# Splitting the last token products of a linear-attention block into a z part and a rest

## Chip, cores and metric

The kernel runs on one core of a Trainium2 chip. The metric is the device time of one launch in microseconds; the median over five runs of the kernel before the change is 197.4 us (196.29 to 198.48). A second number, the span, is the time between the first and the last instruction of one profiled execution; it is a little shorter than the time of the same run.

The engines are named as in the profile: PE is the matrix engine (PEld its weight loads), DVE the vector engine, ACT the scalar engine, POOL GpSimd, SP the engine whose queue issues the DMAs here.

## What is computed

A transformer layer on 2048 tokens of width 448: linear attention with 16 heads of 28, then a gated feed-forward part of width 1792. Both have a layernorm in front and a residual around them.

```python
qkv = (x_norm @ wqkv).reshape(B, S, 3, H, Dh)          # H = 16, Dh = 28
phi = lambda t: jnp.where(t > 0, t + 1, jnp.exp(t)) + 1e-6
pq, pk = phi(q), phi(k)
kv  = jnp.einsum("bhsd,bhse->bhde", pk, v)
z   = jnp.einsum("bhsd->bhd", pk)                      # sum of phi(K) over the tokens
num = jnp.einsum("bhqd,bhde->bhqe", pq, kv)
den = jnp.einsum("bhqd,bhd->bhq", pq, z)[..., None] + 1e-6
h   = x + (num / den) @ wo
h2  = h + (gelu(hn @ w_gate) * (hn @ w_up)) @ w_down   # hn = layernorm(h)
```

Softmax is absent, so all tokens share one 28x28 matrix per head (kv) and one vector z. Both are sums over all tokens: nothing of the attention's output can be formed before the last K tile has gone through phi.

## The kernel before

The 2048 tokens are 16 tiles of 128. Every tile passes through the same named steps; a number behind a name is its tile.

**First layernorm.** bnst1 and bnag1 (DVE) form mean and variance, ln1 and rstd1 (ACT) the reciprocal root, normD (DVE, tiles 0 to 3) or normP (POOL, the others) the normalised tile `xnn`, in a ring of six slots. Each slot is 512 wide: 448 columns of data and 64 columns that hold ones. Tiles 0 to 3 are transposed by PE (tr), the others by a DMA that SP issues (xT).

**Projections.** k and q are four matmuls of 448 columns each. ek, ck and pk (ACT, DVE, DVE) make phi(K), in a ring of four slots; eq and rq (ACT) are the exponential and the relu of Q, cq and aq (DVE) join them to phi(Q). K and Q share four PSUM banks in turn.

**Token products.** V is never formed. For every K tile, four matmuls accumulate xnn^T phi(K) into four banks (4 to 7), each with another 128 rows of xnn as weights (pt). The last of these, number 3, covers data columns 384 to 447 and the 64 columns of ones: its lower half is z, repeated over 64 partitions. For tiles 0 to 14 the four are one task (`pt4`), issued in the order 3, 0, 1, 2. For tile 15 there are two tasks: `pt1_15`, number 3 alone, and `pt3_15`, the other three.

**From the sums to gate/up.** z1 (ACT) and z0 (DVE) spread z over 128 partitions; evpA and evpD bring the four token products to SBUF; kv (PE, 16 matmuls) multiplies them by the V weights, kvm (DVE) masks the heads, w2 (PE, four) multiplies by wo, evwA and evwD evict. In parallel, per tile: t1 = phi(Q) * z (t1d on DVE for tile 0, t1p on POOL otherwise, two buffers), dr the sum over each head (DVE), deA the epsilon (ACT), rd the reciprocal (DVE), pn the scaled phi(Q) (DVE). Tiles 0 and 1 are then transposed on PE (tro, evicted by evo), the other pairs by a DMA (oT). out1 and out2 multiply by w2, hr (DVE) adds x. A second layernorm (bnst2, bnag2; ln2 and rstd2 on ACT for tiles 0 and 1, negm2, vpe2 and pow2 on POOL otherwise; nhD or nhP) and a transpose (trh for tiles 0 and 1, elsewhere wr64 or wrap on DVE and the DMA hT) give the input of the feed-forward part.

**Feed-forward.** gu2 and gu4 are groups of gate and up matmuls that fill one bank each; ge (ACT) is the gelu, hm (DVE) the product. down (14 matmuls of 448 columns) follows for each tile, fo (DVE) adds the residual and do (SP) writes out. The w_down load (`dwd`) is issued by SP among the transposes. The table of gelu is loaded on ACT (tbl2) after the last exponential of Q.

**Order.** The order of the tasks on each engine is not the order in which the program creates them. It is written out as five lists of task numbers (`ORDERS`, lines 15 to 51; PE, ACT, DVE, POOL, SP); `_Graph.place` (line 110) takes them and `_Graph.emit` (line 145) issues each engine's tasks in that order, with a semaphore wait for every dependence on another engine. An engine that waits holds up whatever stands behind in its list. Before the change, PE's list around the edit reads, by names: k_13 q_4 k_14 q_5 k_15 pt4_11 pt4_12 pt4_13 pt4_14 pt1_15 pt3_15 q_7 q_6 kv q_8 w2_1 w2_0 q_11 w2_3 q_9 w2_2 tro_0 q_10 tro_1 out1_0 out1_1 q_15 q_12 q_13 q_14 trh_0 trh_1 out2_2 gu2_0. DVE's after the last pk: aq_0 cq_4 aq_4 cq_5 aq_5 evpD_3 z0 t1d_0 evpD_2 dr_0 dr_1 rd_0 kvm dr_2 evwD_1 dr_3 rd_2 rd_1 pn_0 pn_1.

Lines of the code that appear in the profile: 407 the K and Q projections, 418 to 420 ek, ck, pk, 426 the token products, 434 and 435 eq and rq, 452 and 453 z1 and z0, 465 kv, 474 w2, 491 t1, 494 dr, 498 pn, 507 tro, 526 out, 532 hr, 553 trh, 563 wrap, 606 and 608 gate and up, 578 down, 626 ge, 628 hm.

Of the kernel before, what the change touches and what calls it, by code (L numbers as in the profile page):

```python
# [5 lines left out]
BF16 = mybir.dt.bfloat16  # L6
F32 = mybir.dt.float32
ALU = mybir.AluOpType
# [4 lines left out]


ORDERS = (
    "30 36 38 70 47 45 67 56 80 54 75 65 88 63 83 74 79 91 120 87 103 95 115 107 130 142 119 154 134 166 146 178"
    " 158 190 170 182 202 214 219 229 234 244 194 206 218 233 248 249 253 250 290 256 294 292 265 298 259 296 314"
    " 262 316 318 319 277 268 271 274 332 336 355 433 438 386 443 448 453 458 417 463 505 510 515 520 525 530 471"
    " 468 489 535 577 582 540 561 587 592 597 602 543 674 607 612 617 622 627 632 637 642 705 647 650 653 721 726"
    " 731 736 741 746 751 756 761 766 771 776 781 786 803 808 656 791 794 797 813 818 823 828 833 838 843 848 853"  # L20
    " 858 863 868 800 873 876 879 882 885",
    "4 29 33 34 37 42 43 51 52 71 46 69 60 61 55 76 68 98 64 90 99 84 125 89 110 126 111 81 92 82 137 138 149 104"
    " 150 161 162 116 185 173 121 131 174 122 143 186 197 224 155 225 198 167 209 239 210 179 240 191 203 215 230"
    " 221 245 235 220 236 284 287 288 254 255 252 307 251 258 311 346 293 266 297 350 315 257 267 317 264 260 261"
    " 278 326 327 263 328 329 378 382 272 279 333 270 273 275 276 269 338 413 436 434 409 439 441 446 444 449 451"
    " 454 456 461 459 464 466 508 506 511 481 513 516 485 518 523 521 526 528 533 553 531 557 536 538 670 666 580"
    " 578 585 583 590 588 593 595 697 600 605 598 603 701 608 610 613 615 620 618 625 623 630 628 633 635 640 638"
    " 645 643 722 724 727 729 732 734 737 739 742 744 747 749 752 754 757 759 762 764 767 769 772 774 777 779 782"
    " 784 787 789 804 806 809 811 816 814 821 819 824 826 829 831 834 836 839 841 846 844 849 851 854 856 861 859"
    " 869 871 864 866",  # L30
    "31 32 40 35 41 49 50 39 44 53 48 72 58 59 73 57 62 96 66 97 123 108 77 124 78 109 183 85 147 86 148 135 93 184"
    " 136 94 159 171 160 105 106 222 207 172 117 223 118 195 132 196 133 208 144 237 145 156 238 157 339 341 168 169"
    " 302 340 180 181 300 192 193 204 205 216 303 217 231 342 232 246 247 301 371 372 373 374 286 285 304 289 306"
    " 310 308 291 345 295 349 347 312 309 313 377 299 351 348 320 352 321 323 322 324 404 325 330 381 331 334 383"
    " 335 379 384 380 337 405 402 356 359 403 412 360 357 408 414 358 361 435 437 415 442 410 440 411 387 447 445"
    " 388 369 476 450 474 452 546 477 475 366 455 457 390 462 460 391 547 548 480 418 549 389 392 465 467 421 419"
    " 509 507 484 420 512 514 422 397 517 519 400 661 423 552 524 522 486 482 487 483 529 428 662 659 556 554 527"
    " 660 472 431 555 558 534 665 532 469 690 669 493 537 539 559 490 692 693 581 491 667 579 584 668 492 586 494"
    " 671 691 672 541 700 562 696 591 495 589 594 596 601 563 565 604 566 599 698 702 606 703 544 675 567 699 609"
    " 564 611 676 614 616 678 621 619 572 626 500 624 631 503 629 677 679 634 636 639 680 709 641 706 644 710 707"  # L40
    " 646 648 711 708 575 688 723 725 728 730 733 735 738 740 743 745 748 719 750 654 753 685 755 758 760 716 763"
    " 765 768 770 651 773 775 778 780 783 785 788 790 810 657 805 807 812 792 798 795 817 815 822 820 825 827 830"
    " 832 835 837 840 842 847 845 850 852 855 857 862 860 865 801 870 872 874 867 877 880 883 886",
    "17 24 0 18 1 23 27 19 2 25 21 22 100 101 112 127 113 128 139 140 151 152 163 187 164 175 176 28 226 199 188"
    " 211 200 212 227 241 26 242 20 305 343 344 375 376 407 406 362 363 364 365 368 478 479 393 394 395 399 550 396"
    " 425 426 424 427 551 430 663 664 695 694 497 498 496 499 502 569 570 568 571 574 682 681 683 687 712 713 714"
    " 718 684 715",
    "3 5 6 7 8 9 10 11 12 13 14 15 16 102 114 129 141 153 165 177 189 201 213 228 243 280 281 282 283 353 385 416"
    " 370 367 354 398 401 488 429 432 560 673 542 470 704 504 501 573 576 545 473 689 720 717 686 649 799 658 793"
    " 875 655 652 802 881 878 884 796 887",  # L50
)


# [117 lines left out]
def bass_sequential_preLN__linear_attn_block__glu_gated_geglu__prompt_kernel(  # L171
    nc, A_x, A_wqkv, A_wo, B_x, B_w_gate, B_w_up, B_w_down, out
):
    S, D, FF, H, DH = 2048, 448, 1792, 16, 28
    T, P = S // 128, S // 256
# [2 lines left out]
    FC = 768  # L178
    NJ = FF // 128
    EPS_LN, EPS = 1e-5, 1e-6  # L180
    XN_R, HN_R, HR = 6, 4, 8
    N_PE_TR = 4
    B1_CHUNKS = [2, 2, 4, 4, 4]
    WARM = 40
# [3 lines left out]
    G = _Graph()  # L188
    es = ExitStack()
    with es:  # L190
        block = es.enter_context(nc.Block())

        def sb(name, shape, dt):
            return es.enter_context(nc.sbuf_tensor(name, shape, dt))

        x_sb = sb("x_sb", [128, T, D], BF16)
        xnn = sb("xnn", [128, XN_R, 512], BF16)
# [23 lines left out]
        ln2 = sb("ln2", [128, T], F32)  # L221
        rs2 = sb("rs2", [128, T], F32)
        e1 = sb("e1", [128, 4, D], BF16)
        pk = sb("pk", [128, 4, D], BF16)
        eq = sb("eq", [128, T, D], BF16)
        pq = sb("pq", [128, T, D], BF16)
        pt_sb = sb("pt_sb", [128, 4, D], BF16)
# [14 lines left out]
        ps = es.enter_context(nc.psum_tensor("ps", [128, 8, 512], F32))  # L242
        psb = ps[:].bitcast(BF16)

        def bufs(name, n):
            return [_Buf("%s%d" % (name, i)) for i in range(n)]

        b_x = bufs("x", T)
        b_xn = bufs("xn", XN_R)
        b_xnT = [bufs("xnT%d_" % t, 2) for t in range(T)]  # L250
        b_ones2 = _Buf("ones2")
# [4 lines left out]
        b_epsd = _Buf("epsd")  # L256
        b_st1, b_mv1, b_nm1, b_ln1, b_rs1 = bufs("st1", T), bufs("mv1", T), bufs("nm1", T), bufs("ln1", T), bufs("rs1", T)
        b_st2, b_mv2, b_nm2, b_ln2, b_rs2 = bufs("st2", T), bufs("mv2", T), bufs("nm2", T), bufs("ln2", T), bufs("rs2", T)
        b_e1, b_pk = bufs("e1", 4), bufs("pk", 4)
        b_eq, b_pq = bufs("eq", T), bufs("pq", T)  # L260
        b_pt, b_z, b_kvm, b_w2 = bufs("pt", 4), bufs("z", 2), _Buf("kvm"), bufs("w2", NG)
        b_t1, b_den, b_rd = bufs("t1", 2), bufs("den", 4), bufs("rd", 4)
# [5 lines left out]
        b_ps = bufs("ps", 8)  # L268
# [3 lines left out]
        BK_PT = (4, 5, 6, 7)  # L272
# [15 lines left out]
        def op(eng, fn, r, w, name, after=()):  # L288
            return G.add(eng, fn, r=r, w=w, name=name, after=after)
# [47 lines left out]
        def act_exp(fn, r, w, name):  # L337
            t_ = G.add("act", fn, r=r, w=w, name=name, after=[tbl1])
            exps.append(t_)
            return t_  # L340
# [58 lines left out]
        def slot():  # L399
            slots[0] += 1  # L400
            return BK_S[slots[0] % 4]

        def proj(e, W, t, bk, w):
            ins = None
            for k in range(4):
                W(k)
                ins = e.matmul(ps[:, bk, 0:D], xnT[:, t, k, :], w[:, k, :], start=(k == 0), stop=(k == 3))  # L407
            return ins

        def proj_reads(t, b):  # L410
            return [(b_xnT[t][0], 0), (b_xnT[t][1], 2), (b[0], 0), (b[1], 3)]

        def k_tile(t):
            bk = slot()
            i = t % 4
            psK = ps[:, bk, 0:D]
            G.add("pe", lambda e, W: proj(e, W, t, bk, wk_sb), r=proj_reads(t, b_wk), w=[b_ps[bk]], name="k_%d" % t, mw=True)
            eks.append(act_exp(lambda e: e.activation(e1[:, i, :], psK, AF.Exp), [b_ps[bk]], [b_e1[i]], "ek_%d" % t))  # L418
            op("dve", lambda e: e.tensor_scalar(e1[:, i, :], e1[:, i, :], 1.0 + EPS, 0.0, ALU.min, ALU.max), [b_e1[i]], [b_e1[i]], "ck_%d" % t)
            op("dve", lambda e: e.scalar_tensor_tensor(pk[:, i, :], psK, EPS, e1[:, i, :], ALU.max, ALU.add), [b_ps[bk], b_e1[i]], [b_pk[i]], "pk_%d" % t)  # L420
            groups = ((3, 0, 1, 2),) if t < T - 1 else ((3,), (0, 1, 2))
            for cs in groups:
                def fpt(e, cs=cs):
                    ins = None
                    for c in cs:
                        ins = e.matmul(ps[:, BK_PT[c], 0:D], xnn[:, t % XN_R, c * 128:(c + 1) * 128], pk[:, i, :], start=(t == 0), stop=(t == T - 1))  # L426
                    return ins
                G.add("pe", fpt, r=[b_xn[t % XN_R], b_ones2, b_pk[i]], w=[b_ps[BK_PT[c]] for c in cs], name="pt%d_%d" % (len(cs), t))


        def q_tile(t):
# [6 lines left out]
        for what in SEQ.split():  # L438
            t = int(what[1:])
# [6 lines left out]
        for i in range(2):  # L446
            cs = slice(0, FC) if i == 0 else slice(FC, FF)
# [25 lines left out]
        for g in range(NG):  # L473
            G.add("pe", lambda e, g=g: e.matmul(ps[0:GW, BK_W2[g], 0:D], kvm[:, g, :], wo_sb[:, g, :], start=True, stop=True),
                  r=[b_kvm, b_wo], w=[b_ps[BK_W2[g]]], name="w2_%d" % g)
# [218 lines left out]
```

## Time and profile before

| what | us |
|---|---|
| median of five runs | 197.4 |
| time of the profiled execution | 197.96 |
| its span | 195.9 |
| PE busy in the span | 188.7 |
| DVE busy in the span | 132.7 |
| gate and up matmuls, line 606, busy (line 608 runs beside it) | 86.7 |
| down matmuls, line 578, busy | 43.4 |

Busy time by stretch of 5 us each:

| stretch, us | PE | DVE | ACT | POOL |
|---|---|---|---|---|
| 15 to 20 | 3.58 | 3.20 | 2.40 | 1.97 |
| 25 to 30 | 5.00 | 4.47 | 2.18 | 2.91 |
| 35 to 40 | 4.99 | 4.35 | 3.67 | 0.93 |
| 40 to 45 | 4.77 | 5.00 | 3.82 | 4.76 |
| 45 to 50 | 4.75 | 5.00 | 4.26 | 0.20 |
| 55 to 60 | 5.00 | 5.00 | 3.40 | 2.79 |
| 80 to 85 | 5.00 | 5.00 | 0.31 | 2.43 |
| 120 to 125 | 5.00 | 2.92 | 0.00 | 1.26 |

In a timeline each line gives the start, the duration, the engine, the source line, the operation, what it writes and reads, how many instructions are merged, and in brackets the idle time of the engine before it with what ended it. The ends of matmuls are modelled and overlap the next start, so a stop of PE is read from the distance between starts; the brackets show only part of it. The granted clock of PE is 1.00 in every stretch.

### The profile page before, as it was taken

The page shows a single profiled execution, that of the slowest core. Times are in us where ns is not written, and L with a number is a line of the kernel's source. Part 1 is how long each engine was busy: PE and PEld are TensorE (multiplying, and loading weights), DVE is VectorE, ACT ScalarE, POOL GpSimd, SP SyncE. Part 2 cuts the span into 40 slices and gives each one's busy share as a digit, 9 for nine tenths or more (in the row PEclk, how much of TensorE's full clock was granted, in tenths as well). Part 3 has the DMA queues.
Part 4 walks back from the last instruction along what each step waited for, and adds up shares of the span by engine and source line. Part 5 has one row for each costly group of instructions (what it writes and reads, how often), then busy time and mean ns, then how long its engine had stood idle before and what let it go on. Part 6 is the DMA issues. An engine that isn't in the chain of part 4 may idle for free.

```text
span 195.9 us, 4160 instructions
## 1 busy us (share of the span) xinstructions
PE 188.7 (96%) x1572; PEld 104.2 (53%) x1572; DVE 132.7 (68%) x355; ACT 77.4 (39%) x226; POOL 51.3 (26%) x93
## 2 busy tenths in 40 slices
PE   7897999999999999999999999999999999999995
PEld 7443455554468697554454635445343544555554
DVE  2896986899999999999777757045653405452422
ACT  3685754688992244222231440044444002443000
POOL 7043751092055475802430412510000000000000
DMA  5989254998222794922401176500350002000022
GB/s 156 290 270 93 60 107 98 231 215 172 54 57 56 119 308 94 95 56 54 100 3 30 25 70 76 132 12 0 62 106 0 0 0 74 0 0 3 0 95 94
DMA packets 35955, 16.97 MB, mean 87 GB/s; under 512 B 27744, under 2 KB 34656, under 8 KB 35936
## 3 DMA queue, kind: packets, MB, share of 16 engines
q1 hardware_dynamic: 35792, 16.60, 40.7%
q8 instruction: 12, 0.20, 0.4%
q10 hardware_dynamic: 144, 0.11, 0.2%
q14 instruction: 7, 0.06, 0.1%
HBM read 8.26 MB, written 1.84 MB: 52 GB/s over the span
## 4 chain that ended last, share of the span: by engine, by line
PE 82%; DVE 8%; DMA 5%; POOL 1%; ACT 1%; issue 1%; SPq 0%; DVEq 0%; POOLq 0%
PE ps L606 29%; PE ps L578 22%; PE ps L608 16%; PE ps L407 6%; PE ps L526 6%; PE ps L426 4%; DMA x_sb<-in_A_x_dram 3%; DMA xnT<-xnn 2%; DVE pqn L498 1%; DVE den L494 1%; DVE st L351 1%; DVE w L479 1%; DVE x_sb L532 1%; DVE pk L420 0%; PE ps L553 0%
## 5 line engine op out<-in xcount | busy, mean ns | idle before, releaser
L608 PE MATMUL ps<-hnT,wgu_sb 64*128 64x512 bf16 (+1 forms) x490 | 87.4, 334 | 0.0
L606 PE MATMUL ps<-hnT,wgu_sb 64*128 64x512 bf16 (+1 forms) x490 | 86.7, 334 | 0.2 <-issue 0.2
L626 ACT ACTIVATE gl<-ps 128x256 bf16<-128x256 f32 x112 | 37.0, 380 | 84.5 <-PE ps L608 81.0
L628 DVE TENSOR_TENSOR hh<-ps,gl 128x256 bf16<-128x256 f32 x112 | 43.4, 415 | 34.1 <-ACT gl L626 33.8
L606 PEld LDWEIGHTS ps<-hnT,wgu_sb 64*128 64x128 bf16 x490 | 44.1, 94 | 21.8 <-issue 2.7
L608 PEld LDWEIGHTS ps<-hnT,wgu_sb 64*128 64x128 bf16 x490 | 42.6, 94 | 15.0 <-DVE hh L628 5.0
L578 PE MATMUL ps<-wd_sb,hh 128*128 128x448 bf16 (+1 forms) x238 | 43.4, 342 | 0.0
L578 PEld LDWEIGHTS ps<-wd_sb,hh 128*128 128x128 bf16 x238 | 22.8, 98 | 20.4 <-issue 1.9
L491 POOL TENSOR_TENSOR t<-pq,zbc 128x448 f32<-128x448 bf16 x15 | 16.6, 1118 | 30.7 <-DVE pq L487 21.9
L351 DVE BATCH_NORM_STATS2 st<-x_sb 128x6 f32<-128x448 bf16 x32 | 19.2, 613 | 3.8 <-DMA x_sb<-in_A_x_dram 3.8
L582 DVE TENSOR_TENSOR x_sb<-ps,x_sb 128x448 bf16<-128x448 f32 (+1 forms) x17 | 10.0, 592 | 15.6 <-PE ps L578 15.6
L407 PE MATMUL ps<-wk_sb,xnT 128*128 128x448 bf16 x64 | 14.4, 353 | 1.9 <-DMA xnT<-xnn 1.4
L407 PE MATMUL ps<-wq_sb,xnT 128*128 128x448 bf16 x64 | 14.2, 353 | 0.3 <-ACT eq L434 0.3
L426 PE MATMUL ps<-pk,xnn 128*128 128x448 bf16 x64 | 13.9, 353 | 0.4 <-DVE pk L420 0.3
L526 PE MATMUL ps<-w,pqnT 112*128 112x448 bf16 x64 | 13.8, 353 | 0.1
L418 ACT ACTIVATE e<-ps 128x448 bf16<-128x448 f32 x16 | 8.7, 543 | 9.7 <-PE ps L407 9.7
L561 POOL TENSOR_SCALAR hn<-x_sb,nm,rs 128x448 bf16<-128x448 bf16 x14 | 11.5, 828 | 3.3 <-DMA hnT<-hn 2.7
L532 DVE TENSOR_TENSOR x_sb<-ps,x_sb 128x448 bf16<-128x448 f32 x16 | 9.7, 613 | 2.2 <-PE ps L526 2.2
L498 DVE TENSOR_TENSOR pqn<-pq,rd 128x448 bf16<-128x448 bf16 x16 | 11.1, 707 | 0.0
L391 POOL TENSOR_SCALAR xnn<-x_sb,nm,rs 128x448 bf16<-128x448 bf16 x12 | 8.6, 714 | 6.9 <-ACT rs L360 5.9
L420 DVE SCALAR_TENSOR_TENSOR pk<-ps,e 128x448 bf16<-128x448 f32 x16 | 9.9, 617 | 0.2
L407 PEld LDWEIGHTS ps<-wk_sb,xnT 128*128 128x128 bf16 x64 | 5.9, 97 | 7.7 <-issue 2.4
(68 smaller groups left out, 136.9 us busy)
## 6 DMA issues: line engine op xcount, KB each, us to landing
out_dram<-x_sb SPq DMA_DIRECT2D x15, 112.0 KB, 1.8
wd_sb<-in_B_w_down_dram SPq DMA_DIRECT2D x1, 1568.0 KB, 7.0
x_sb<-in_A_x_dram SPq DMA_DIRECT2D x3, 448.0 KB, 6.4
wgu_sb<-in_B_w_gate_dram SPq DMA_DIRECT2D x1, 896.0 KB, 11.9
wgu_sb<-in_B_w_up_dram SPq DMA_DIRECT2D x1, 896.0 KB, 15.8
wgu_sb<-in_B_w_gate_dram SPq DMA_DIRECT2D x1, 672.0 KB, 5.9
wgu_sb<-in_B_w_up_dram SPq DMA_DIRECT2D x1, 672.0 KB, 8.3
wo_sb<-in_A_wo_dram SPq DMA_DIRECT2D x1, 392.0 KB, 9.3
```

Of the source, the lines that this page charges most:

```text
L351: op("dve", lambda e: e.bn_stats(st[:, t, :], src_ap), [b_src], [b_st[t]], "bnst%s_%d" % (tag, t))
L407: ins = e.matmul(ps[:, bk, 0:D], xnT[:, t, k, :], w[:, k, :], start=(k == 0), stop=(k == 3))
L426: ins = e.matmul(ps[:, BK_PT[c], 0:D], xnn[:, t % XN_R, c * 128:(c + 1) * 128], pk[:, i, :], start=(t == 0), stop=(t == T - 1))
L491: op(eng, lambda e, t=t, n=n: e.tensor_tensor(t1[:, n, :], pq[:, t, :], zbc[:, :], ALU.mult), [b_pq[t]] + b_z, [b_t1[n]], "t1%s_%d" % (eng ...
L498: op("dve", lambda e, t=t, n=n, i=i, i2=i2: e.tensor_tensor(pqn[:, i2, n, :, 0:GW].rearrange("p g (h d) -> p g h d", h=4), pq[:, t, :].rea ...
L526: ins = e.matmul(ps[:, BK_OUT[n], 0:D], pqnT[0:GW, i2, n, g, :], w2[:, g, :], start=(g == 0), stop=(g == NG - 1))
L532: op("dve", lambda e, t=t, bo=bo: e.tensor_tensor(x_sb[:, t, :], ps[:, bo, 0:D], x_sb[:, t, :], ALU.add), [b_ps[bo], b_x[t]], [b_x[t]], "h ...
L578: ins = e.matmul(psO, hh[:, j, (t % HR) * 128:(t % HR + 1) * 128], wd_sb[:, j, c0:c1], start=(j == 0), stop=(j == NJ - 1))
L606: e.matmul(psG[:, jj * N:(jj + 1) * N], wgu_sb[A_, k, j * 128:(j + 1) * 128], hnT[A_, ka_, c0:c0 + N], start=(k == 0), stop=(k == NK - 1))
L608: ins = e.matmul(psU[:, jj * N:(jj + 1) * N], wgu_sb[B_, k, j * 128:(j + 1) * 128], hnT[B_, kb_, c0:c0 + N], start=(k == 0), stop=(k == NK ...
L626: G.add("act", lambda e, gi=gi, cs_=cs_, psG=psG: e.activation(gl[:, gi, cs_], psG[:, cs_], AF.Gelu_apprx_tanh), r=[b_ps[BK_G[i]]], w=[b_g ...
L628: op("dve", lambda e, dst=dst, srcU=srcU, srcL=srcL: e.tensor_tensor(dst, srcU, srcL, ALU.mult), [b_ps[BK_U[i]], b_glh], [b_ar[j_][t % HR] ...
```

## The change

Three things change. For tiles 10 to 15 the four token-product matmuls become two tasks, as tile 15 had them before: number 3, with z in it, and the other three. To let the second task run later, the rings that it reads grow: `xnn` from six to ten slots, `pk` from four to eight. And the five lists of `ORDERS` are all written anew, for every engine and over the whole program. The added tasks shift the task numbers, so the lists differ nearly everywhere as numbers.

```diff
-    XN_R, HN_R, HR = 6, 4, 8
+    XN_R, PK_R, HN_R, HR = 10, 8, 4, 8
+    PT_SPLIT = 10
...
-        pk = sb("pk", [128, 4, D], BF16)
+        pk = sb("pk", [128, PK_R, D], BF16)
...
         def k_tile(t):
             bk = slot()
-            i = t % 4
+            i, ip = t % 4, t % PK_R
...
-            op("dve", lambda e: e.scalar_tensor_tensor(pk[:, i, :], psK, EPS, e1[:, i, :], ALU.max, ALU.add), [b_ps[bk], b_e1[i]], [b_pk[i]], "pk_%d" % t)
-            groups = ((3, 0, 1, 2),) if t < T - 1 else ((3,), (0, 1, 2))
+            op("dve", lambda e: e.scalar_tensor_tensor(pk[:, ip, :], psK, EPS, e1[:, i, :], ALU.max, ALU.add), [b_ps[bk], b_e1[i]], [b_pk[ip]], "pk_%d" % t)
+            groups = ((3, 0, 1, 2),) if t < PT_SPLIT else ((3,), (0, 1, 2))
...
-                        ins = e.matmul(ps[:, BK_PT[c], 0:D], xnn[:, t % XN_R, c * 128:(c + 1) * 128], pk[:, i, :], start=(t == 0), stop=(t == T - 1))
+                        ins = e.matmul(ps[:, BK_PT[c], 0:D], xnn[:, t % XN_R, c * 128:(c + 1) * 128], pk[:, ip, :], start=(t == 0), stop=(t == T - 1))
```

The new lists by names, where the prediction speaks of them (`...` marks parts left out):

```
PE    ... k_4 pt4_3 k_5 k_6 pt4_4 k_7 pt4_5 ... k_12 k_13 q_4 k_14 pt4_9 k_15 pt1_10 q_5 pt3_10
      pt1_11 pt1_12 pt1_13 pt1_14 pt1_15 pt3_11 pt3_12 pt3_13 pt3_14 pt3_15 q_7 q_9 kv q_6
      w2_1 w2_2 w2_3 w2_0 q_8 tro_0 q_11 tro_1 out1_0 q_10 out1_1 q_13 q_15 q_12 q_14
      trh_0 trh_1 out2_2 gu2_0 gu2_1 out2_4 gu2_2 ... gu2_5 out2_6 gu2_6 gu2_7 down448_0 gu2_9
      gu2_8 gu2_11 gu2_10 out2_8 down448_1 gu2_12 gu2_13 gu4_14 gu4_15 gu4_16 out2_10 down448_3 ...
DVE   ... pk_15 aq_3 aq_4 cq_5 aq_5 z0 t1d_0 dr_0 evpD_3 rd_0 evpD_2 dr_1 pn_0 dr_2 rd_1 kvm dr_3
      evwD_1 evwD_3 rd_2 rd_3 pn_1 pn_3 dr_4 pn_2 hr_0 cq_6 bnst2_0 hr_1 ... hr_4 hm1_2 hm0_2 hr_5 wrap_3 ...
ACT   ... rstd1_7 ln1_10 rstd1_8 ek_4 ... z1 deA_0 evpA_0 evpA_1 deA_1 eq_7 rq_7 ...
SP    ... dwg0 dwu0 dwg1 dwu1 oT_1 oT_2 dwd oT_3 hT_3 hT_2 hT_4 oT_4 hT_5 hT_7 hT_6 ...
```

In SP's list before the change, `dwd` stands after oT_3, hT_3 and hT_2; in PE's list before, down448_1 and down448_0 stand after gu2_12, ahead of out2_8 and gu2_13.

## The prediction

> **What bounds the kernel now.** I read the page first (busy shares, then the span in 40 slices), because it says which engine a change has to help; then the timeline of PE over the stretch that the edit touches, because busy shares hide short stops; then the timelines of DVE, POOL and ACT there, to see what each stop waits for.
>
> ```profile
> PE 188.7 (96%) x1572; PEld 104.2 (53%) x1572; DVE 132.7 (68%) x355; ACT 77.4 (39%) x226; POOL 51.3 (26%) x93
> ...
> PE   7897999999999999999999999999999999999995
> ...
> DVE  2896986899999999999777757045653405452422
> ```
>
> PE has work in every slice after the first four, so no other engine can be worth much by itself; only PE's stops can be won. DVE is full from slice 9 to 19 (about 40 to 95 us), so in that stretch PE runs at the pace at which DVE hands it operands and frees its banks.
>
> ```profile
> 34.53 3.95 PE L426 MATMUL ps<-pk,xnn 128*128 128x448 bf16 x20
> 38.31 1.68 PE L407 MATMUL ps<-wq_sb,xnT 128*128 128x448 bf16 x8
> 40.23 1.03 PE L465 MATMUL ps<-pt_sb,wv_sb 128*112 128x112 bf16 x16 [0.24 <-DVE pt_sb L459]
> ...
> 44.63 0.92 PE L407 MATMUL ps<-wq_sb,xnT 128*128 128x448 bf16 x4
> 45.74 0.43 PE L507 MATMUL ps<-ident,pqn 128*112 128x128 bf16 x4 [0.18 <-DVE pqn L498]
> 46.01 2.06 PE L526 MATMUL ps<-w,pqnT 112*128 112x448 bf16 x8
> 47.90 2.44 PE L407 MATMUL ps<-wq_sb,xnT 128*128 128x448 bf16 x12
> 50.64 0.93 PE L407 MATMUL ps<-wq_sb,xnT 128*128 128x448 bf16 x4 [0.30 <-ACT eq L434]
> 51.41 1.11 PE L553 MATMUL ps<-ident,hn 128*128 128x128 bf16 x14
> ```
>
> Read these by the distance from one start to the next: four matmuls of 448 columns take 0.76 us back to back (one per 0.19). Eight Q matmuls from 38.31 should hand over at 39.82; kv starts at 40.23, so 0.41 is lost. In the same way 0.35 is lost before the second transpose (45.74), 0.38 inside the eight at 46.01 (1.89 where 1.51 is needed), 0.47 inside the twelve at 47.90 (2.74 against 2.27), and about 0.6 in small pieces around kv, w2 and the transposes. Together some 2.2 us between the last token product and the first gate/up matmul, which starts at 53.97. Before it, PE is gapless from 17.62 (k_4) to 39.82 but for 0.27 ahead of pt4_4, which waits for pk_4.
>
> ```profile
> 37.94 0.54 ACT L452 ACTIVATE zbc<-ps 64x448 f32<-64x448 f32 x1 [1.30 <-PE ps L426]
> ```
> ```profile
> 38.59 0.39 DVE L453 COPY zbc<-zbc 64x448 f32<-64x448 f32 x1
> 39.02 0.63 DVE L491 TENSOR_TENSOR t<-pq,zbc 128x448 f32<-128x448 bf16 x1
> ...
> 43.75 1.93 DVE L498 TENSOR_TENSOR pqn<-pq,rd 128x448 bf16<-128x448 bf16 x2
> ```
> ```profile
> 40.78 4.42 POOL L491 TENSOR_TENSOR t<-pq,zbc 128x448 f32<-128x448 bf16 x4 [0.24 <-DVE den L494]
> ```
>
> The chain behind those stops begins with z: the last pt1 matmul (37.55), its eviction z1 on ACT (37.94), its copy z0 on DVE (38.59), the products with z (t1), the sums, reciprocals, pn, tro, evo, out1, hr, the second layernorm, trh, gate/up. In the chain of waits DVE links of this sort are what interrupts PE between 38 and 51.
>
> **The change, part by part.**
>
> *Split of the token products.* No matmul is added: six tiles of four become one plus three. PE's semaphore waits grow by five tasks; the split task that exists before (pt1_15, pt3_15) starts at 37.55 and 37.74, exactly a matmul apart, so I charge 0.
>
> *z earlier.* In the new order PE runs k_4 to k_15, pt4_3 to pt4_9, q_4, pt1_10, q_5, pt3_10, then pt1_11 to pt1_15, and only then pt3_11 to pt3_15. k_4 stays at 17.62: it is released by the transposed x tile 4, which lands at 17.48, 0.58 after the wo load ahead of it in the queue. From there to pt1_15 there are 19 groups before k_15 plus k_15 and q_5 (21 x 0.757 = 15.9) and pt1_10, pt3_10 and four pt1 (1.5): pt1_15 starts at 35.03 instead of 37.55. With the offsets of today (0.39 to z1, 0.65 on to z0) z1 is at 35.42 and z0 at 36.07: 2.5 us earlier. The five pt3 after it (5 x 0.57) keep PE busy until 38.06, then q_7 and q_9 until 39.58. pk_15 must be there by 35.0: k_15 starts at 32.0, and ek_15, ck_15, pk_15 need 0.9 + 0.5 + 0.3 + 0.6, so 34.1 to 34.3. That PE is not stopped before needs the x tiles: SP issues a transpose every 1.25 us, k tiles with their pt come every 1.51. On ACT rstd1_8 now stands ahead of ek_4, so tile 8 is issued right behind tile 7 (19.1 instead of 20.04); tiles 10 to 15 then land (2.45 after issue) 0.4 to 0.9 us before their k. pk_4 is no longer waited for, since k_6 is put ahead of pt4_4: 0.27 won.
>
> *What now queues behind waits.* DVE stands idle about 0.8 us in front of z0. On ACT deA_0 stands between z1 and the evictions evpA and waits for dr_0, to 37.65; pt3_15 is not done before 38.06, which covers it; without that cover kv would be late by the same. normD_3 on DVE now stands behind bnst1_4 and bnst1_5, which wait for the x load of 10.14: the last PE transposes move from 10.9 to 11.9 and PE reaches the end of pt4_2 at 17.2 instead of 16.0, still ahead of 17.62. The ones column of ten xnn slots instead of six makes that memset some 0.25 longer by its row (0.36); it is over near 2.5, its reader starts at 5.42: 0. The wider rings cost no time.
>
> *The stage itself, at today's start-to-start steps* (dr, pn, hr, evictions on DVE 0.53; rd 0.16; nhD 0.3; ACT 0.44; eviction to product as today). DVE: z0 36.07, t1d 36.50, dr_0 37.04, evpD_3 37.57, evpD_2 38.26, dr_1 38.80, pn_0 39.33, dr_2 39.86, kvm 40.63 (kv starts 39.58, 1.05 after it), dr_3 41.18, evwD_1 41.76, evwD_3 42.30, pn_1 43.15, pn_3 43.67, pn_2 44.72, hr_0 45.25, hr_1 46.76, nhD_0 48.2, wr64_0 49.35, wr64_1 49.6. PE: w2 41.33, tro_0 42.85, tro_1 43.88, out1_0 44.15 (just behind evo_0, 43.47 to 44.06), out1_1 45.66, the four Q to 49.46, trh_0 49.57, out2_2 50.33, first gate/up 51.95. Stops left: about 0.15 at w2 and 0.3 around trh. First gate/up 2.0 us earlier than 53.97. The gelu table load moves with it: the Q evictions end at 53.2 instead of 55.4.
>
> *Transposes and loads.* pqn for tiles 2, 3 is issued at 45.3, where the four gate/up loads (issued about 30.0 instead of 31.6, done at 49.5 today) are still in flight; I let it land near 49, for a reader at 50.33. The w_down load is moved ahead of oT_3, hT_3 and hT_2 (SP order): 7.0 us from about 52.3. It may hold oT_2 to 55.2, its reader is due 55.11: 0 to 0.2. hT_2 would land at 65.0 for a reader at 66.24; today it lands at 68.56 and its reader starts at 68.65.
>
> *DVE-bound stretch, same walk.* It begins 2.0 us earlier and has the same instructions; hr_5 is put ahead of the wraps, which takes away the 0.31 before out2_6, and hT_2 is early, which takes away 0.39 before gu2_7: gu2_7 at 66.24 instead of 68.65. down448_0 then stands where PE would wait for hm. The set that ends before gu4_14 ends at 84.1 instead of 86.6. Beyond, DVE has room (6 tenths and less from slice 20), the transposed tiles 8 to 15 come many us early, and PE's work is fixed: whatever is won by 84 stays. Sum: -2.0 to -2.5.
>
> *A rule against it.* The trace: pn_1 took 1.45 us (43.75 to 45.68 with pn_0, where 0.56 each is usual) while t1 of tile 5 ran on POOL from 43.77 to 45.20; the wrap at 78.36 took 1.10 beside POOL. The Trainium skill, page "SBUF — State Buffer", section "SBUF: two separate sides", says that VectorE and GpSimd take their shared port pair as an exclusive lock: a DVE operation with two SBUF inputs, such as pn, or in a two-port mode, waits for the whole GpSimd operation or the other way round. The rows agree (delays 0.5 to 0.9), except that pn_0 beside the same row took 0.56, having come first or in the seam. Today's lock hits pn_1; in the new order POOL's t1 run ends at 42.9 and pn_1 comes at 43.15, clear, while pn_0 (39.33) stands at the start of t1 for tile 3 (dr_1 frees its buffer at 39.41). By the rule alone, the loser waits up to 1.0: if it is pn_0, kvm moves to about 41.1 and the gain falls by 0.45. By the row of pn_0, nothing. A coin's toss: I take 0.2 off.
>
> Result: -2.1 us. Span 195.9 - 2.1 = 193.8; the profiled run's own time is 197.96, so 195.9 on that run's scale; the median shown is 197.40, 0.56 less: **195.3 us**.
>
> **The rivals.** *Gain eaten in the DVE-bound stretch* (22%): if the new sequence there costs some 0.3 at five or six hm hand-overs (today's PE stops of this sort: 0.31, 0.39, 0.33), or oT_1 waits for the loads, 0.7 to 1.5 of the gain remains unwon: about 196.6. For it: DVE at 9 tenths; slacks in my walk of 0.05 to 0.4. Against it: PE has downs and outs there as cover.
>
> *The chain doesn't shorten* (11%): z is early but kv needs pt3_15 as before (38.06 against 38.31), and w2 and out1 hang on kv, not on z: then only 0.3 + 0.27 is won, 196.9. For it, kvm is bound by kv in my walk. Against: dr, rd and pn have no more to share DVE with evictions after w2.
>
> *Slower by the port lock* (15%): if the t1 run slips by more than the 0.25 of clearance and then stays in step with DVE, each of pn_1, pn_3, pn_2, pn_4, pn_5 and the wraps can lose 0.9 on a full DVE. Today's trace pays about four such delays (pn_1, two wraps, pn_10). The gain is gone at about two or three more, and with six, 6 x 0.9 - 2.1 = +3.3, so 200.5; near 199.5 with five. Against it: the next t1 waits for aq_6, near 52, long after these pn.
>
> **How the numbers follow.** About 1% (2.0 us) is what a measurement of this kernel can tell from no change, and my sum lies on that line. Likeliest case 52%, 194.2 to 196.2, of which some four fifths reach 195.4 given what the walk finds at gu4_14 (2.5 before the lock). Eaten or not shortened, 33%, almost all within 1%. Slower 15%, all but a trace beyond +1%. So faster 0.42, same 0.43, slower 0.15. The range 193.9 to 198.4 leaves out the upper part of the lock case and a thin tail below.
>
> **What would show it.** z1 near 35.4 and z0 near 36.1; L426 ending with fifteen matmuls that start near 35.2; kv near 39.6; first gate/up at 52.0 and hT_2 landing before gu2_7. Wrong, if k_10 to k_15 wait for xnT, if L498 rows of 1.4 us multiply, if out2_2 waits for pqnT, or if PE's stops between 57 and 85 grow past today's 2 us.

## The result, and the profile after

The changed kernel takes 196.32 us (median of 43 runs, 195.45 to 197.32), the kernel before 197.11 us in the larger set of runs (80, 196.13 to 199.07). The ratio is 0.9952, 95% interval 0.9938 to 0.9966: faster by about half a per cent, a gain of 0.8 to 1.0 us where 2.1 were forecast. By the line of 1% that the prediction drew, this counts as the same (0.43 there) and not as faster (0.42); the interval, 0.3% wide, is finer than that line. The profiled execution took 197.0 us with a span of 195.3, against 197.96 and 195.9.

First the page of the changed kernel: busy time by engine, then PE and DVE in 40 slices. Source lines are one higher than before the change.

```profile
PE 188.2 (96%) x1572; PEld 104.3 (53%) x1572; DVE 131.2 (67%) x355; ACT 77.3 (40%) x226; POOL 52.1 (27%) x93
...
PE   7699999999999999989999999999999999999994
...
DVE  3698978899999997999777557146443306453412
```

The page looks as before. It cannot show a gain of this size, nor where a part of it was lost. The timeline of PE over the stage that was changed can:

```profile
34.44 4.51 PE L427 MATMUL ps<-pk,xnn 128*128 128x448 bf16 x23
38.79 1.68 PE L408 MATMUL ps<-wq_sb,xnT 128*128 128x448 bf16 x8
40.30 0.99 PE L466 MATMUL ps<-pt_sb,wv_sb 128*112 128x112 bf16 x16
...
43.79 0.92 PE L408 MATMUL ps<-wq_sb,xnT 128*128 128x448 bf16 x4
44.55 0.39 PE L508 MATMUL ps<-ident,pqn 128*112 128x128 bf16 x4
44.88 0.93 PE L527 MATMUL ps<-w,pqnT 112*128 112x448 bf16 x4
...
47.16 3.19 PE L408 MATMUL ps<-wq_sb,xnT 128*128 128x448 bf16 x16
50.19 0.94 PE L554 MATMUL ps<-ident,hn 128*128 128x128 bf16 x14
50.97 1.68 PE L527 MATMUL ps<-w,pqnT 112*128 112x448 bf16 x8
52.58 0.28 PE L607 MATMUL ps<-hnT,wgu_sb 64*128 64x256 bf16 x1
```

Read it by the starts again. Eight Q matmuls take 1.51 (38.79 to 40.30): the stop of 0.41 before kv is gone. Sixteen take 3.03 (47.16 to 50.19), sixteen times 0.19: the 0.47 is gone. From the first of these Q matmuls (q_7) to the first gate/up it is now 13.79 us, and it was 15.66. Why, the timelines of ACT and DVE say: z1 and z0 start while PE still works off token products.

```profile
36.15 0.54 ACT L453 ACTIVATE zbc<-ps 64x448 f32<-64x448 f32 x1 [0.54 <-PE ps L427]
```
```profile
36.72 0.39 DVE L454 COPY zbc<-zbc 64x448 f32<-64x448 f32 x1 [0.24 <-ACT zbc L453]
37.15 0.62 DVE L492 TENSOR_TENSOR t<-pq,zbc 128x448 f32<-128x448 bf16 x1
```

I cut the span at five tasks and took the distances from the start of one to the start of the next. The table holds nine of the fourteen profiles, those of experiments that come below among them, since most of these touch only one stretch:

| kernel | k_4 starts | k_4 to q_7 | q_7 to first gate/up | to gu4_14 | to gu4_28 | rest |
|---|---|---|---|---|---|---|
| before | 17.62 | 20.69 | 15.66 | 32.64 | 39.92 | 69.40 |
| before, second profile | 15.79 | 21.06 | 15.66 | 32.59 | 39.93 | 69.41 |
| changed | 17.38 | 21.41 | 13.79 | 32.22 | 41.08 | 69.40 |
| changed, second profile | 17.41 | 21.09 | 13.80 | 32.22 | 41.08 | 69.41 |
| no filler (changed, pt3 behind pt1) | 16.33 | 21.37 | 16.04 | 32.22 | 41.08 | 69.41 |
| pn ahead of dr_13 | 17.20 | 21.37 | 13.81 | 32.53 | 40.66 | 69.41 |
| and deA_13 later | 16.90 | 21.03 | 13.80 | 32.22 | 40.22 | 69.38 |
| filler in the old order | 16.04 | 21.18 | 15.49 | 33.43 | 39.92 | 69.42 |
| split alone, old order | 15.88 | 21.78 | 15.67 | 33.43 | 39.92 | 69.43 |

Of the five left out, three are kernels of the table with layernorm 4 forward and have the same columns from q_7 on, within 0.02; the other two have down ahead of out. These columns repeat mostly to 0.02 us between executions of one order; the first two do not, and vary by more than the whole gain. So the change wins 1.87 in its stage, 0.4 in the stretch behind it, and gives 1.15 back between gu4_14 and gu4_28. In the first pair of profiles the front gives 0.24 and the K tiles take 0.72, but that pair does not speak for the kernels: the place of k_4 differs by 1.83 between two profiles of the same kernel.

Where the 1.15 begins is seen in rows of PE, DVE, POOL and ACT, all of the changed kernel:

```profile
85.74 0.39 PE L609 MATMUL ps<-hnT,wgu_sb 64*128 64x512 bf16 x1 [0.56 <-DVE hh L629]
```
```profile
82.50 0.60 DVE L495 TENSOR_REDUCE den<-t 128x16 f32<-128x448 f32 x1
83.02 1.99 DVE L499 TENSOR_TENSOR pqn<-pq,rd 128x448 bf16<-128x448 bf16 x2
84.94 0.74 DVE L629 TENSOR_TENSOR hh<-ps,gl 128x256 bf16<-128x256 f32 x2
...
86.36 0.73 DVE L629 TENSOR_TENSOR hh<-ps,gl 128x256 bf16<-128x256 f32 x2
```
```profile
83.18 2.73 POOL L492 TENSOR_TENSOR t<-pq,zbc 128x448 f32<-128x448 bf16 x2 [3.11 <-DVE den L495]
```
```profile
83.48 0.66 ACT L627 ACTIVATE gl<-ps 128x256 bf16<-128x256 f32 x2
```

PE waits in the middle of its gate/up work for hm. Two pn (pn_11, pn_10) take 1.99 us where two take 1.15 elsewhere; the second has 1.46 by itself. POOL works on t1 of tile 15 from 83.18 to 84.54 beside it, released by the dr just ahead of the pn. This is the delay that the prediction calls the port lock, at a place that it did not price: gu4_14 to gu4_15 is 2.25 us instead of 1.51. The gelu is not what hm waits for here, since both of its rows are over at 84.14 and hm starts at 84.94.

### The profile page after: what moved, and what is told of

Its sections match the earlier page's. It is cut to its first block, busy times and chain, and to the rows that moved or that the text cites. A ratio compares the mean times of both kernels' runs of the same rounds, so it can differ in the third digit from the quotient of the medians.

```text
span 195.3 us, 4142 instructions
## 1 busy us (share of the span) xinstructions
PE 188.2 (96%) x1572; PEld 104.3 (53%) x1572; DVE 131.2 (67%) x355; ACT 77.3 (40%) x226; POOL 52.1 (27%) x93
## 3 DMA queue, kind: packets, MB, share of 16 engines
HBM read 8.26 MB, written 1.84 MB: 52 GB/s over the span
## 4 chain that ended last, share of the span: by engine, by line
PE 81%; DVE 5%; DMA 3%; POOL 0%; issue 0%; ACT 0%; ACTq 0%; DVEq 0%; POOLq 0%
PE ps L607 25%; PE ps L579 21%; PE ps L609 17%; PE ps L408 8%; PE ps L527 6%; PE ps L427 4%; DMA xnT<-xnn 3%; DVE pqn L499 1%; DVE hh L629 1%; DVE x_sb L533 1%; DVE den L495 1%; DVE pq L488 1%; DVE eq L487 1%; PE ps L475 0%; PE ps L466 0%
## 5 line engine op out<-in xcount | busy, mean ns | idle before, releaser
L629 DVE TENSOR_TENSOR hh<-ps,gl 128x256 bf16<-128x256 f32 x112 | 42.7, 413 | 36.1 <-ACT gl L627 34.0
L492 POOL TENSOR_TENSOR t<-pq,zbc 128x448 f32<-128x448 bf16 x15 | 17.1, 1153 | 27.2 <-DVE pq L488 13.7
L499 DVE TENSOR_TENSOR pqn<-pq,rd 128x448 bf16<-128x448 bf16 x16 | 10.4, 672 | 0.0
L364 POOL TENSOR_SCALAR ln<-mv 128x2 f32<-128x2 f32 x7 | 1.5, 221 | 30.8 <-DVE mv L353 30.7
```

The lines of the kernel that those rows point to most:

```text
L492: op(eng, lambda e, t=t, n=n: e.tensor_tensor(t1[:, n, :], pq[:, t, :], zbc[:, :], ALU.mult), [b_pq[t]] + b_z, [b_t1[n]], "t1%s_%d" % (eng ...
L499: op("dve", lambda e, t=t, n=n, i=i, i2=i2: e.tensor_tensor(pqn[:, i2, n, :, 0:GW].rearrange("p g (h d) -> p g h d", h=4), pq[:, t, :].rea ...
L629: op("dve", lambda e, dst=dst, srcU=srcU, srcL=srcL: e.tensor_tensor(dst, srcU, srcL, ALU.mult), [b_ps[BK_U[i]], b_glh], [b_ar[j_][t % HR] ...
```

## The experiments

The kernels that follow change the order of tasks only (and, for the last two orders, the split in the old kernel). Diffs are in task names. Ratios are to the kernel before, with 95% intervals.

**No filler in the new order.** On PE each pt3 stands behind its pt1 again.

```diff
 PE: ... q_5 pt3_10
-pt1_11 pt1_12 pt1_13 pt1_14 pt1_15 pt3_11 pt3_12 pt3_13 pt3_14 pt3_15
+pt1_11 pt3_11 pt1_12 pt3_12 pt1_13 pt3_13 pt1_14 pt3_14 pt1_15 pt3_15
```

> The changed kernel with one thing undone on PE alone: each pt3 of tiles 11 to 15 stands directly behind its pt1 again, so z is formed after the token products, as before the change; all other orders stay. Theory that the early z is what opened the stage: z1 moves from 36.15 to about 38.4 and z0 with it (2.3 later), DVE idles 2 us more, the first gate/up starts near 54.2 to 54.6 instead of 52.58, ratio 0.998 to 1.005. Rival, the order of DVE after z is what helped: kv still starts near 40.3 and the first gate/up loses under 0.7, ratio at most 0.998.

Measured 1.0075 (1.0047 to 1.0103). PE's timeline of this kernel, then two rows of ACT:

```profile
33.35 4.51 PE L427 MATMUL ps<-pk,xnn 128*128 128x448 bf16 x23
37.70 1.68 PE L408 MATMUL ps<-wq_sb,xnT 128*128 128x448 bf16 x8
41.05 1.00 PE L466 MATMUL ps<-pt_sb,wv_sb 128*112 128x112 bf16 x16 [1.68 <-DVE pt_sb L460]
...
43.04 0.96 PE L475 MATMUL ps<-wo_sb,kvm 112*112 112x448 bf16 x4 [0.23 <-DVE kvm L470]
```
```profile
39.64 0.31 ACT L497 ACTIVATE den<-den,eps_d 128x16 f32<-128x16 f32 x1 [1.77 <-DVE den L495]
39.98 0.98 ACT L458 ACTIVATE pt_sb<-ps 128x448 bf16<-128x448 f32 x2
```

Two Q groups should end at 39.21; kv starts at 41.05, 1.84 later, because the evictions that it reads stand behind the work on z in the new orders: evpD_2 on DVE behind z0, t1d and dr (over at 40.77), and evpA on ACT behind deA_0, which waits for dr_0. The second is over at 40.96 and so ends the wait, though the bracket names DVE; the prediction had said of deA_0 that kv would be late by it without the cover of pt3_15. Without the early z the new order is worse than the old (16.04 against 15.66 for the stage), and the time lies above what was expected (1.005 at most). The filler is worth 2.2 us inside it.

**The filler in the old order.** The split and the rings, the old order on every engine, but for these moves:

```diff
 PE: k_15
-pt1_11 pt3_11 pt1_12 pt3_12 pt1_13 pt3_13 pt1_14 pt3_14 pt1_15 pt3_15
+pt1_11 pt1_12 pt1_13 pt1_14 pt3_11 pt3_12 pt1_15 pt3_13 pt3_14 pt3_15
 DVE: aq_5
-evpD_3 z0 t1d_0 evpD_2
+z0 t1d_0 evpD_3 evpD_2
```

> The orders of the kernel before, with the split of tiles 10 to 15 and the larger rings, and only these moves: on PE pt1_11 to pt1_14, pt3_11, pt3_12, pt1_15, pt3_13 to pt3_15 behind k_15, on the vector engine z0 and t1d_0 ahead of evpD_3. Theory: the filler needs DVE to be free when z arrives; here DVE still works off aq and cq to 37.8, so z0 moves only from 38.6 to about 37.9, the first gate/up gains 0.3 to 0.7, ratio 0.996 to 0.999. Rival, the early z alone gives all: first gate/up 1.5 us or more earlier, ratio 0.992 or less.

Measured 0.999 (0.9956 to 1.0024). The stage gains 0.17 us, less than even the low expectation. Early z and the order that can use it are one change: the order alone loses 0.4, the filler alone gains 0.2. (This filler is not quite the same: three pt3 stand behind pt1_15 here, five in the changed kernel.)

**The split alone.** The old order, each pt4 of tiles 10 to 14 replaced by pt1 and pt3 in its place.

```diff
 PE:
-k_15 pt4_11 pt4_12 pt4_13 pt4_14
+k_15 pt1_11 pt3_11 pt1_12 pt3_12 pt1_13 pt3_13 pt1_14 pt3_14
```

> The kernel before with the split of tiles 10 to 15 and the larger rings, pt1 and pt3 of each tile adjacent and every order as it was. Theory: the split and the rings by themselves cost nothing, ratio 0.999 to 1.001, and the token products at line 427 keep their 0.19 us steps. Rival: five more waits on PE or the longer memset cost 0.1 us each, ratio 1.002 or more.

Measured 0.9992 (0.9961 to 1.0022), with the stage at 15.67: the split and the rings cost nothing in the stage, and nothing that the timed runs can tell. The profiles have one open point. Both kernels with the split in the old order take 33.43 us from the first gate/up to gu4_14, where the old kernel takes 32.64 and 32.59. The difference of 0.8 is one stop of PE, in front of out2_4: the transpose that it reads (oT_2) lands 4.7 us after its issue in both, and 3.1 in both profiles of the old kernel. Why is not settled. A loss of 0.8 in every run would be above the interval, which ends at 0.4.

**The port lock.** In the changed kernel, pn_11 and pn_10 ahead of the dr that releases t1 of tile 15.

```diff
 DVE: hm0_11
-dr_13 pn_11 pn_10 hm0_12
+pn_11 pn_10 dr_13 hm0_12
```

> The changed kernel with one move on the vector engine: pn_11 and pn_10 stand ahead of dr_13 instead of behind it, so that they run before the POOL product of tile 15 (released by dr_13) can hold the shared port. Port-lock theory: the pn_10 row falls from 1.46 to about 0.6 us, hm of group 13 ends about 0.7 earlier, the PE distance from gu4_14 to gu4_15 goes from 2.25 to about 1.55, span 194.6, ratio to the kernel before 0.9915. Rival, the gelu or the PE queue holds gu4_15 back: the distance stays at 2.2, ratio 0.995. Rival, oT_5 or another reader becomes late in its place: the stop moves to out2_10 and the ratio stays at 0.995.

Measured 0.9941 (0.9916 to 0.9966): not told apart from the changed kernel. DVE and ACT of this kernel:

```profile
82.30 1.14 DVE L499 TENSOR_TENSOR pqn<-pq,rd 128x448 bf16<-128x448 bf16 x2
83.36 0.60 DVE L495 TENSOR_REDUCE den<-t 128x16 f32<-128x448 f32 x1
84.61 0.76 DVE L629 TENSOR_TENSOR hh<-ps,gl 128x256 bf16<-128x256 f32 x2 [0.65 <-ACT gl L627]
```
```profile
84.00 0.31 ACT L497 ACTIVATE den<-den,eps_d 128x16 f32<-128x16 f32 x1 [1.92 <-DVE den L495]
84.22 1.30 ACT L627 ACTIVATE gl<-ps 128x256 bf16<-128x256 f32 x4
```

The lock is gone (two pn in 1.14), and a new wait has its place: hm now waits for the gelu, and the gelu stands on ACT behind deA_13, which waits for the dr that I had moved back. The theory of the lock held, but its price did not come back: the move put dr_13, and with it what queues behind deA_13, 1.07 us later, counted from the first gate/up. PE gets 0.42 back behind gu4_14 and loses 0.31 in front of it.

**Lock and new wait.** The same, and on ACT:

```diff
 ACT: deA_12
-deA_13 ge0_12 ge1_12
+ge0_12 ge1_12 deA_13
```

> The changed kernel with pn_11 and pn_10 ahead of dr_13 as in the first experiment, and deA_13 on the scalar engine moved behind ge1_12, so that the gelu of group 12 does not wait for the later dr_13. Theory: that wait is what took the place of the port lock; hm0_12 starts near 83.9 instead of 84.6, the two PE stops at gu2_13 and gu4_14 (0.35 and 0.33 in the first experiment, 0.78 together in the changed kernel) fall below 0.2 together, and gu4_14 to gu4_28 shrinks from 41.1 to about 40.4 us. Rival: PE frees and refills the banks at the pace of hm in any case, the stop moves to gu4_15 or gu4_16 and the distance stays above 40.9.

Measured **0.9888** (0.9848 to 0.9928), 195.42 us: faster than both kernels, 0.8 to 0.9 us below the medians of the changed one (196.25 and 196.32). ACT and DVE:

```profile
82.63 0.66 ACT L627 ACTIVATE gl<-ps 128x256 bf16<-128x256 f32 x2 [1.20 <-PE ps L609]
83.35 0.31 ACT L497 ACTIVATE den<-den,eps_d 128x16 f32<-128x16 f32 x1
```
```profile
81.64 1.15 DVE L499 TENSOR_TENSOR pqn<-pq,rd 128x448 bf16<-128x448 bf16 x2
82.71 0.61 DVE L495 TENSOR_REDUCE den<-t 128x16 f32<-128x448 f32 x1
83.24 0.74 DVE L629 TENSOR_TENSOR hh<-ps,gl 128x256 bf16<-128x256 f32 x2
```

The gelu now waits for PE alone, gu4_14 to gu4_15 is 1.51, and gu4_14 to gu4_28 is 40.22. On DVE the dr and the two pn take 1.60 us up to hm (81.64 to 83.24), and took 2.44 in the changed kernel (82.50 to 84.94). Of the 1.15 us, 0.86 is thus the lock on pn_10 and what queued behind it. deA_13 was not moved by itself; in the changed kernel the gelu behind it is 0.8 us early, so it can hardly hold anything there. The other 0.30 against the old order stays open. It arises at the two places where an out and a down stand together; the next experiment was meant for it.

**Down ahead of out.** In the changed kernel:

```diff
 PE:
-gu4_16 out2_10 down448_3 gu4_17   ...   gu4_21 out2_12 down448_2 gu4_22
+gu4_16 down448_3 out2_10 gu4_17   ...   gu4_21 down448_2 out2_12 gu4_22
```

> The changed kernel with two exchanges on PE: down448_3 ahead of out2_10 and down448_2 ahead of out2_12, as such pairs stand before the change. Theory that the step from gate/up to out costs about 0.3 us where the step to down costs 0.1 to 0.2: the stops of 0.32 at gu4_16 and 0.38 at gu4_21 fall to 0.1 to 0.2 and each triple from about 0.5 to 0.3 in all; gu4_14 to gu4_28 shrinks by 0.3 to 0.4. Rival, the stop there is a wait for data (oT or hr) that the order cannot mend: it reappears unchanged in front of out2_10 and out2_12.

Measured 1.0183 (1.0139 to 1.0226), slower by some 5 us than the changed kernel. DVE's timeline says why:

```profile
89.61 0.59 DVE L583 TENSOR_TENSOR x_sb<-ps,x_sb 128x448 bf16<-128x448 f32 x1
90.12 0.82 DVE L629 TENSOR_TENSOR hh<-ps,gl 128x256 bf16<-128x256 f32 x2
94.63 0.62 DVE L533 TENSOR_TENSOR x_sb<-ps,x_sb 128x448 bf16<-128x448 f32 x1 [3.69 <-PE ps L527]
```

hr_10 stands in DVE's list where out2_10 used to come early; now it holds the queue for 3.69 us, and the hm of the next gate/up groups stand behind it. PE stops for 1.45 and 2.05 there. (down448_3 also waits 1.1, for the bank that the fo at 89.61 frees.) I had left DVE's list as it was, so the exchange shows what that costs and not what the step between gate/up and out is worth: the question is not answered.

**Layernorm 4 forward.** In the changed kernel, to mend the wait of k_6 for its transpose (0.45 in the first profile):

```diff
 DVE: bnst1_4
-bnst1_5 bnag1_4
+bnag1_4 bnst1_5
 ACT: rstd1_3
-eq_1 ek_1 ln1_4 ek_2 evxA_3 rstd1_4
+ln1_4 rstd1_4 eq_1 ek_1 ek_2 evxA_3
```

> The changed kernel with layernorm 4 moved forward: bnag1_4 directly behind bnst1_4 on the vector engine, ln1_4 and rstd1_4 ahead of eq_1 on the scalar engine. Theory of the missed DMA slot: normP_4 ends near 12.3 instead of 13.7, the transpose of tile 4 is issued before the queue fills, its issue takes 1.3 instead of 2.4 us, tile 6 is issued near 16.5 instead of 17.5 and all later ones 1 us earlier; the stops of 0.45 before k_6 and 0.53 before k_10 go, z1 starts near 35.4 instead of 36.15, ratio to the kernel before about 0.991. Rival, SP is held until the wo load has drained whatever was issued before: tile 6 stays at 17.5, ratio 0.995. Rival, the moved ACT work delays k_3 and q_3: k_4 slips past 17.4 by up to 0.4 and eats a part.

Measured 0.9967 (0.9944 to 0.999). The transpose of tile 4 was issued at 12.22 and that of tile 6 at 15.42, earlier still than expected, and the stop before k_6 is gone. But tile 4 landed at 17.08 all the same, 4.86 us after its issue, k_10 then waited 0.57, and the median did not move. Together with the first mend of the lock:

> Both moves in the changed kernel, pn_11 and pn_10 ahead of dr_13 and layernorm 4 forward. If the two losses are independent they add: 0.75 and 0.9 us, span about 193.6, ratio to the kernel before 0.987. If the earlier start of the whole chain shifts DVE and POOL against each other again, one of the two is lost and the ratio is 0.991.

0.9964 (0.994 to 0.9987): nothing added. Together with all mends, the exchange of down and out among them:

> All mends together in the changed kernel: layernorm 4 forward, pn ahead of dr_13 with deA_13 later, down ahead of out twice. If each works by itself: from k_4 to gu4_28 about 1.5 us less than in the changed kernel (108.5), near 107.0, span 193.5 with an equal start of k_4, ratio to the kernel before 0.988. If the median stays at the changed kernel's 0.995, the stops that a profile shows are not those of the median run.

1.0184 (1.013 to 1.0239), the exchange's loss again. And upon the best kernel:

> The best kernel so far (pn ahead of dr_13, deA_13 behind ge1_12) with layernorm 4 forward as well. If the wait of k_6 for its transpose costs the median run 0.45 us, as the profile of the changed kernel shows it, the ratio falls from 0.989 to about 0.987, and from k_4 to gu4_28 it is 106.8 to 107.3 us against 107.3. Rival: the transposes run ahead until the one that meets the instruction load and PE waits there instead; then the ratio stays at 0.989.

0.9902 (0.9865 to 0.9938), 195.27 us, not distinct from 0.9888: no gain of the early layernorm can be told, and the rival, that PE waits at a later tile instead, holds (0.55 before k_10, 0.01 before k_6).

**Both kernels again.**

> The changed kernel unaltered, to have it beside the others on one chip and to see a second profile. From k_4 to gu4_28 it should again take 108.5 us within 0.3 whatever k_4 itself does (16.3 to 17.7 in the profiles so far, moving with the landing of the wo load, 14.7 to 16.9); gu4_14 again keeps PE 0.75 us too long; ratio 0.995. If instead k_4 is what differs between kernels, its place should repeat at 17.4.

0.9936 (0.9913 to 0.9959); 108.19 from k_4 to gu4_28, and the 0.75 at gu4_14 again. k_4 repeats at 17.41, as the rival said, but kernels with the same front have it at 16.33 to 17.20.

> The kernel before unaltered, for a second profile. If the place of k_4 is set by how the first loads land and not by the kernel, it lies somewhere between 16.0 and 17.7 instead of at 17.62, and from k_4 to gu4_28 it takes 108.9 us within 0.3.

k_4 lies at 15.79 instead of 17.62, with 109.24 from there to gu4_28, both just outside what was expected; the execution took 196.21 us instead of 197.96.

## Why the prediction came out as it did

The sign was right and the time lies in the range, but the likeliest case, 2.1 us, did not come true; what came is near the case called "gain eaten", 196.6. That nearness is in part luck: the case had small losses at five or six hm, and what came is one large loss at one hm, while the K tiles won nothing. With that hm mended the kernels take 195.42 and 195.27 us, where the prediction had the changed one (195.3). By its steps:

- *z earlier, and the stage at today's steps.* The walk had 16.92 us from pt1_15 to the first gate/up (35.03 to 51.95). In the profile pt1_15 starts at 35.76, so the stage took 16.82. The mechanism and its price are right, and the runs without filler and with filler alone show that both the filler and the new order of DVE and ACT are needed. The rival "the chain doesn't shorten" falls.
- *pn_0 beside the t1 of tile 3.* pn_0 paid nothing: it took 0.61, having started 0.16 ahead of that t1 (40.06 and 40.22). pn_1, which paid before (1.45), took 0.57. The 0.2 that I took off for it was not due.
- *The DVE-bound stretch.* 0.5 was expected and 0.42 came: 0.34 at gu2_7, ahead of which hT_2 now lands (66.26 against 66.81), and 0.12 at out2_6.
- *"Whatever is won by 84 stays": this step failed.* I had listed pn_10 among today's delays and never asked what covers it. In the old order it lies beside two downs and an out, 28 down matmuls from 78.15, then out2_8 to 85.07, so PE needed no hm:

```profile
78.15 5.47 PE L578 MATMUL ps<-wd_sb,hh 128*128 128x448 bf16 x28
83.46 1.68 PE L526 MATMUL ps<-w,pqnT 112*128 112x448 bf16 x8
```
```profile
82.38 1.46 DVE L498 TENSOR_TENSOR pqn<-pq,rd 128x448 bf16<-128x448 bf16 x1
```
```profile
81.29 2.06 POOL L491 TENSOR_TENSOR t<-pq,zbc 128x448 f32<-128x448 bf16 x2 [0.92 <-DVE pq L487]
```

In the new order one down has moved ahead, and when the same lock hits pn_10 at 83.56, PE is inside gate/up and lives from hm. Behind q_7 the changed kernel has only two DVE rows of this kind (pn_10 and a cq of 1.12) where the old one had four, and still loses more by them: 1.15 in this stretch, of which the mended kernel shows 0.86 to be this one.
- *The K tiles.* The 0.27 won at pt4_4 was booked against a timetable in which every x transpose lands 2.45 us after its issue. In both profiles of the changed kernel tile 10 needs 3.1 and 3.5, and k_10 waits 0.53 and 0.66 for it. The slack that I had given the tiles was 0.4 to 0.9. That k_10 to k_15 wait for xnT was the first of the signs of being wrong, and it came. From k_4 to q_7 nothing is won: 21.41 and 21.09 against 20.69 and 21.06.
- *k_4 stays at 17.62.* The premise was a single execution. In the four profiles of the old front it is at 15.79 to 17.62, in the six of the changed front at 16.33 to 17.41, later by 0.7 in the mean. Whether the change costs something here, as these few profiles hint, the timed runs don't settle.
- *The lock as a rival that makes it slower* had the right mechanism and the wrong place (pn_1 to pn_5), and came only once.

The sum of the columns from q_7 on is -1.87 - 0.4 + 1.15 = -1.1 us; the two timed ratios, 0.9952 and 0.9936, are -0.9 and -1.3 of 197.1. That fits if the front costs nothing on average. It is not settled: the spans of the four profiles (195.9 and 194.4 before, 195.3 and 195.0 after) do not show the gain, because of the place of k_4.

## What to carry to other kernels

When a reordering moves filler from one place to another, look for the delays that the filler used to hide, at both places: a stall that the trace shows as harmless has a price as soon as its cover goes. An order is a property of all engines at once: an early result gains nothing while its consumer's queue is busy, and moving one task on one engine can make a wait on another the new bound. Cut the span at tasks and compare the distances over several profiles; a stretch that repeats to 0.02 us can be judged from one profile, the start of this kernel cannot.

## What was not expected of the hardware

The packets in the trace that load instructions (on queue 8 and queue 14 by the page) seem to disturb DMA transposes. In eleven of fourteen profiles such a packet starts between 13.6 and 15.3 us; there the transpose of tile 4 lands 3.2 to 5.1 us after its issue. In the other three (the old kernel's second profile, the split alone, the filler in the old order) none starts between 13 and 20, and it lands after 2.5 to 2.6. These three have the earliest k_4 of all (15.79 to 16.04); their packets come at 20.6 to 22.3, and there tile 9 or 10 needs 3.1 to 4.3. In the same manner tile 10 needs 2.7 to 3.5 us in all ten profiles of the new front, where a packet starts between 22.8 and 24.3, while in the old kernel's first profile a packet falls at 23.87 and tile 10, under way since 23.36, is not late (2.4). So not every such packet delays a transpose. That the load delays the transpose is an inference from their times; no experiment moved it, and it isn't settled why the same program loads at 14.95 in one execution and at 21.98 in another.
